# Second filter half transposed by the DMA engines instead of TensorE, and the first half's first inverse step cut into 64-row matmuls

## The chip, the cores and the metric

One core of one Trainium2 chip runs the whole program in one launch. The metric is the device time of one execution in microseconds (us), the median of several runs. The core has five instruction queues that run beside one another and meet only through semaphores: TensorE (PE, matmuls; its weight loads are listed apart as PEld), VectorE (DVE), ScalarE (ACT), GpSimd (POOL) and SyncE (SP), which here only issues DMA transfers. Each queue runs strictly in the order in which the program wrote it.

## What is computed

Two blocks, A and B, are each applied twice to an array x of 2048 rows and 512 channels that starts as `A_q`.

```python
def _A_ref(q, k, v, shift_k, ssm_k, ssm_D):
    k_shift = sum over t of k_pad[:, t:t + S, :] * shift_k[:, ks - 1 - t]     # 4 taps along the rows
    kv = k_shift * v
    y = irfft(rfft(kv padded to 2 S) * rfft(ssm_k padded to 2 S))[:S]         # causal convolution, per channel
    y = y + kv * ssm_D
    return q * y
x = x + _A_ref(_layernorm(x), A_k, A_v, A_shift_k, A_ssm_k, A_ssm_D)
x = x + _B_ref(_layernorm(x), B_w1, B_b1, B_w2, B_b2)     # layernorm, 512 -> 1376, gelu, 1376 -> 512
... the same two lines once more
```

Only `q` depends on x. The convolution result y depends on k, v and the filter `ssm_k` alone, so the kernel computes it once and uses it in both layers.

## The kernel before

**Two halves.** The 2048 rows are two halves of 1024. The program names things with `_0` and `_1` for the halves. y of the first half needs the first half of kv and the first half of the filter. y of the second half needs both halves of both. So the first half's y is ready early, and its two layers (13 smaller blocks of rows in all are worked through, 9 of them for the first half) run while the second half's convolution is still being computed.

**The convolution** is a Fourier transform written as matmuls, in two factors. The tags in the code are:

- `ht0`, `ht1`: the filter half, loaded with channels on the partitions, is turned so that rows lie on the partitions. `turn` (lines 556 to 568) does this: for each of four blocks of 128 channels, 8 TensorE transposes (line 561) into PSUM and one eviction by ACT or DVE.
- `h1_0`, `h1_1`: first factor of the filter's transform (`stage1`, lines 570 to 581): 8 tiles of 16 matmuls, weights of 64 columns, one eviction each (ACT or DVE).
- `h2_0`: second factor (`stage2`, line 590), 8 tiles. Each is evicted into the region HH, and `swap` (lines 594 to 601) copies HH with even and odd partitions exchanged into HI, by 8 DMAs of 256 KB on SP.
- `fir0` to `fir3`: the 4-tap filter of the first half, matmuls on a turned copy of k in region `R_KT`, times v (DVE, line 641).
- `x1_0`, `x2_0`: the two factors for kv, and the products with HH and HI (DVE, line 475, 16 instructions of 128x1024).
- `i1_0`, `i2_0`: the two inverse factors (`inverse1`, line 695; `inverse2`, line 717). `inverse1(..., split)` has two forms. Unsplit: per tile 16 matmuls with 128 rows of weights and 128 columns out. Split: 32 matmuls with 64 rows and 64 columns, two of them on different row halves of the array. The first half used the unsplit form, the second half (`i1_1`) the split one.
- `h2_1`, `p2`, `kt`, `fir4` to `fir7`, `x1_1`, `x2_1`, `sum`, `i1_1`, `i2_1`: the second half. `kt` turns k by 8 DMA transposes straight from DRAM (line 800).

**The layers** per block of rows: `q*` (statistics on DVE line 831, a small chain on POOL lines 836 to 846, a normalization on ACT line 856 or DVE line 857), `y*` (two DVE products and sums), `z*` (the same for the second layernorm, then a transpose, on TensorE for the first two blocks, by DMA after that, line 900), `m1` (line 920, gelu on ACT line 925), `m2` (line 954, added to x on DVE line 958).

**The order** is not found at run time. `SEQ` is a list of all 1187 operations in the order in which they are dealt to the engines' queues; `ENGS` holds one letter for every operation that may run on more than one engine; `BANKS` holds the PSUM bank of every tile. `arrange` reads the three, and `sync` sets the semaphore waits that the data need. A transfer in the SP queue that waits for its data holds back every transfer behind it.

The region `R_HP1`, which receives the turned second filter half, is the same memory as `R_KT`, so it may be written only after the `fir` matmuls of the first half have read it. `R_Y0` is written by `inverse2` of the first half and is free before.

Of the kernel before, what the change touches and what calls it, by code (L numbers as in the profile page):

```python
# [12 lines left out]
PE, ACT, DVE, POOL, SP = "tensor", "scalar", "vector", "gpsimd", "sync"  # L13
# [23 lines left out]
class Prog:  # L37
# [361 lines left out]
def bass_interleave_layers__ssm_conv_h3__mixer_channel_mlp__prompt_kernel(  # L399
        nc, A_q, A_k, A_v, A_shift_k, A_ssm_k, A_ssm_D, B_x, B_w1, B_b1, B_w2, B_b2, out):  # L400
    P = Prog(nc)
# [593 lines left out]
```

## Time and profile before

| | |
|---|---|
| time, median of 3 runs | 236.08 us (235.6 to 236.17) |
| profiled execution, first to last instruction | 234.0 us |
| granted TensorE clock, mean | 1.000 |
| PE busy | 222.7 us, 95% |
| DVE busy | 178.7 us, 76% |
| ACT busy | 164.5 us, 70% |
| POOL busy | 55.5 us, 24% |
| DMA queue of SP | 24.36 MB, 39.7% of 16 engines' span |

The page gives no other time for the profiled execution than its span; the median of the runs shown is 2.08 us above that span. Busy shares are averages over stages that have different limits, so they are read here by stretches of time. A PE that counts as busy isn't necessarily at its peak rate.

### The profile page before, as it was taken

How to read it: one execution, taken by the hardware profiler on the slowest of the kernel's cores; microseconds unless marked ns; L12 is line 12 of the kernel's file. 1: busy time of each engine (PE TensorE's matmuls, PEld its weight loads, DVE VectorE, ACT ScalarE, POOL GpSimd, SP SyncE). 2: the span in 40 equal slices, each digit the busy share in tenths (PEclk: the TensorE clock that was granted, in tenths of full speed). 3: DMA queues.
4: the chain of work that ended last, by engine and by line, in shares of the span. 5: the costliest groups of instructions: out<-in, count | busy, mean ns of one | idle time of the engine just before them, and what ended most of it. 6: DMA issues, size and time to landing. Idle time of an engine off the chain costs nothing.

```text
span 234.0 us, 6498 instructions
## 1 busy us (share of the span) xinstructions
PE 222.7 (95%) x2743; PEld 147.1 (63%) x2765; DVE 178.7 (76%) x362; ACT 164.5 (70%) x262; POOL 55.5 (24%) x113
## 2 busy tenths in 40 slices
PE   7989887999999999999999999999999999999995
PEld 3878776967868596677966576644444444444454
DVE  0699998999999999999999988781777569410222
ACT  2789999989968688999879986488058216802710
POOL 2270132006403405639303331204011120200000
PEclk9999999999999999999999999999999999999999
DMA  6999489928994360033500313401300130170202
GB/s 185 381 386 305 147 229 274 324 65 150 144 211 126 70 158 3 1 48 72 155 4 3 90 24 68 134 3 22 69 0 3 28 62 0 23 115 0 90 0 92
DMA packets 40106, 24.93 MB, mean 107 GB/s; under 512 B 23591, under 2 KB 33677, under 8 KB 40077
## 3 DMA queue, kind: packets, MB, share of 16 engines
q1 hardware_dynamic: 39778, 24.36, 39.7%
q8 instruction: 22, 0.36, 0.7%
q10 hardware_dynamic: 298, 0.16, 0.4%
q14 instruction: 8, 0.06, 0.1%
HBM read 13.23 MB, written 2.10 MB: 66 GB/s over the span
## 4 chain that ended last, share of the span: by engine, by line
PE 58%; DVE 24%; ACT 10%; issue 2%; POOL 2%; DMA 2%; SPq 0%; DVEq 0%
PE ps L920 23%; PE ps L954 23%; DVE ar L475 13%; ACT ar L480 9%; PE ps L695 4%; DVE sm L831 3%; PE ps L590 2%; DMA ar<-in_A_ssm_k_dram 2%; DVE ar L672 2%; DVE ar L958 2%; DVE ar L641 2%; PE ps L717 1%; POOL sm L836 1%; PE ps L578 1%; PE ps L635 1%
## 5 line engine op out<-in xcount | busy, mean ns | idle before, releaser
L925 ACT ACTIVATE ar<-ps,sm 128x256 bf16<-128x256 f32 (+5 forms) x143 | 65.7, 523 | 33.2 <-PE ps L920 32.9
L920 PE MATMUL ps<-ar 128*128 128x256 bf16 (+5 forms) x569 | 81.9, 297 | 0.4 <-ACT ar L480 0.2
L480 ACT ACTIVATE ar<-ps 128x1024 bf16<-128x1024 f32 (+3 forms) x77 | 71.1, 998 | 11.0 <-PE ps L578 3.4
L954 PE MATMUL ps<-ar 128*128 128x512 bf16 (+1 forms) x323 | 75.9, 379 | 1.5 <-issue 0.6
L920 PEld LDWEIGHTS ps<-ar 128*128 128x128 bf16 (+1 forms) x572 | 52.9, 100 | 27.5 <-ACT ar L480 1.1
L475 DVE TENSOR_TENSOR ar<-ar 128x512 bf16<-128x512 bf16 (+2 forms) x104 | 62.7, 646 | 1.5 <-ACT ar L480 0.8
L954 PEld LDWEIGHTS ps<-ar 128*128 128x128 bf16 (+1 forms) x341 | 32.4, 98 | 35.3 <-ACT ar L925 0.4
L958 DVE TENSOR_TENSOR ar<-ar,ps 128x512 bf16<-128x512 bf16 x31 | 20.8, 680 | 32.9 <-PE ps L954 32.9
L831 DVE BATCH_NORM_STATS2 sm<-ar 128x6 f32<-128x512 bf16 x64 | 42.5, 685 | 0.5
L856 ACT ACTIVATE ar<-ar,sm 128x512 bf16<-128x512 bf16 x39 | 30.6, 813 | 12.9 <-DVE sm L843 8.8
L836 POOL TENSOR_SCALAR sm<-sm 128x2 f32<-128x2 f32 (+2 forms) x22 | 9.9, 449 | 89.0 <-DVE sm L832 88.8
L838 POOL TENSOR_TENSOR sm<-sm 128x2 f32<-128x2 f32 (+2 forms) x26 | 21.7, 834 | 25.1 <-DVE sm L836 23.1
L590 PE MATMUL ps<-ar 128*128 128x64 bf16 x512 | 18.4, 193 | 1.5 <-DVE ar L481 0.7
L578 PE MATMUL ps<-ar 128*64 128x128 bf16 x512 | 17.9, 221 | 1.8 <-ACT ar L480 1.2
L590 PEld LDWEIGHTS ps<-ar 128*128 128x128 bf16 x512 | 16.8, 98 | 3.6 <-DVE ar L481 1.3
L578 PEld LDWEIGHTS ps<-ar 128*64 128x64 bf16 x512 | 14.9, 110 | 4.8 <-ACT ar L480 1.9
L481 DVE CAST ar<-ps 128x1024 bf16<-128x1024 f32 x12 | 14.6, 1218 | 1.2 <-PE ps L578 0.9
L846 POOL TENSOR_SCALAR sm<-sm 128x1 f32<-128x1 f32 x34 | 15.1, 460 | 1.6
L695 PE MATMUL ps<-ar 64*128 64x64 bf16 (+1 forms) x384 | 12.4, 203 | 1.0 <-DVE ar L475 0.9
L695 PEld LDWEIGHTS ps<-ar 64*128 64x128 bf16 (+1 forms) x384 | 11.8, 113 | 2.2 <-DVE ar L475 1.0
L857 DVE TENSOR_SCALAR ar<-ar,sm 128x512 bf16<-128x512 bf16 x25 | 10.3, 415 | 2.7 <-POOL sm L846 2.5
L788 DVE SCALAR_TENSOR_TENSOR ar<-ar,sm,ps 128x512 bf16<-128x512 bf16 x16 | 11.1, 740 | 0.3 <-PE ps L590 0.3
(45 smaller groups left out, 93.5 us busy)
## 6 DMA issues: line engine op xcount, KB each, us to landing
ar<-ar SPq DMA_DIRECT2D x16, 256.0 KB, 4.0
ar<-tab_s SPq DMA_DIRECT2D x9, 256.0 KB, 6.3
ar<-in_A_ssm_k_dram SPq DMA_DIRECT2D x8, 256.0 KB, 5.9
ar<-in_A_q_dram SPq DMA_DIRECT2D x8, 256.0 KB, 4.4
ar<-in_A_v_dram SPq DMA_DIRECT2D x8, 256.0 KB, 5.0
out_dram<-ar SPq DMA_DIRECT2D x7, 256.0 KB, 2.5
ar<-in_B_w_dram SPq DMA_DIRECT2D x4, 344.0 KB, 5.2
ar<-in_B_w_dram SPq DMA_DIRECT2D x5, 256.0 KB, 5.2
```

What stands on the lines that cost most here:

```text
L475: return P.op(eng, lambda e: e.tensor_tensor(o, a, b, op), dur, reads=[a, b] + list(more), writes=[o])
L480: return e.activation(dst, src(), AF.Copy)
L578: r = e.matmul(Q(tl, 64 * ri, 64, i * 128, [1, 128]), w, m, start=True, stop=True)
L590: r = e.matmul(Q(tl, 0, 128, i // 8 * 512 + i % 8 * 4, [32, 16], [1, 4]), w, m, start=True, stop=True)
L695: r = e.matmul(Q(tl, 0, 128, i, *([32, 16], [1, 4]) if split else ([1, 128],)), w, m, start=n == 0, stop=n == 1)
L831: P.op(DVE, lambda e, sj=sj, x=x: e.bn_stats(sj, x), 600.0, reads=[x], writes=[sj])
L838: P.op(POOL, lambda e: e.tensor_tensor(r, v, hf, ALU.pow), 420.0 + 149.0 * n, reads=[v, hf], writes=[r])
L856: return e.activation(o, x, AF.Identity, bias=u, scale=r)
L920: r = e.matmul(Q(tl, 0, rows, 0, [1, w]), a, m, start=dk == 0, stop=dk == 3)
L925: P.op(ACT, lambda e, dst=dst, tl=tl, rows=rows, bias=bias, w=w: e.activation(dst, Q(tl, 0, rows, 0, [1, w]), AF.Gelu_apprx_tanh, bias=bia ...
L954: r = e.matmul(Q(tl, 0, 128, 0, [1, 512]), ins[fc][0], ins[fc][1], start=fc == 0, stop=fc == 10)
L958: P.op(DVE, lambda e, x=x, tl=tl: e.tensor_tensor(x, x, Q(tl, 0, 128, 0, [1, 512]), ALU.add), 604.0, reads=[x], writes=[x], tile=tl)
```

## The change

Three things are changed.

1. **The second filter half is turned by DMA.** `load_h(1)` becomes 8 loads of 64 channels (128 KB each) instead of 4 of 128 channels, with the channels of a block dealt to the partitions in another order. The 32 TensorE transposes and four evictions of `ht1` go. In their place, POOL copies each block of 128 channels (128x1024) so that rows with the same remainder modulo 8 lie together, and 8 DMA transposes on SP (64x1024 each) turn the copies from `R_Y0` into `R_HP1`. The weights of `h1_1` are then read with a step of 8 elements between columns instead of 1.
2. **`i1_0` uses the split form.**
3. **One of the eight `spread` operations may run on POOL too, and `SEQ`, `ENGS` and `BANKS` are new.** There are now 1195 operations.

```diff
     def load_h(half, o):
         for b in range(4):
-            dma(A(0, 128, o + b * 1024, [1, 1024]), dr(A_ssm_k, b * 128 * 2048 + 1024 * half, [2048, 128], [1, 1024]), 1 << 18, paced=True)
+            if 1 and half:
+                for i in range(2):
+                    dma(A(64 * i, 64, o + b * 1024, [1, 1024]), dr(A_ssm_k, (b * 128 + 64 * i) * 2048 + 1024, [2048, 8], [8 * 2048, 8], [1, 1024]), 1 << 17, paced=True)
+            else:
+                dma(A(0, 128, o + b * 1024, [1, 1024]), dr(A_ssm_k, b * 128 * 2048 + 1024 * half, [2048, 128], [1, 1024]), 1 << 18, paced=True)
...
-            P.op(BOTH, f, {ACT: 912.0, DVE: 395.0}, reads=[c, m], writes=[o])
+            P.op((ACT, DVE, POOL), f, {ACT: 1040.0, DVE: 395.0, POOL: 2850.0}, reads=[c, m], writes=[o])
...
     load_h(1, R_HRAW1)
     P.tag = "ht1"
-    turn(1, R_HRAW1, R_HP1)
+    P.tag = "hcopy"
+    for b in range(4):
+        o, x = A(0, 128, R_Y0 + 1024 * b, [128, 8], [1, 128]), A(0, 128, R_HRAW1 + 1024 * b, [1, 8], [8, 128])
+        P.op(POOL, lambda e, o=o, x=x: e.tensor_copy(o, x), 2080.0, reads=[x], writes=[o])
+    P.tag = "ht1"
+    for b in range(4):
+        for i in range(2):
+            x, o = A(64 * i, 64, R_Y0 + 1024 * b, [1, 1024]), A(0, 128, R_HP1 + 1024 * b + 512 * i, [64, 8], [1, 64])
+            P.op(SP, lambda e, x=x, o=o: e.dma_start_transpose(o, x), 1300.0, reads=[x], writes=[o], dma=True, nbytes=1 << 17)
+    lhs = lambda g: A(0, 128, R_HP1 + 512 * (g // 8) + g % 8, [8, 64])
     P.tag = "h1_1"
-    stage1(lambda g: A(0, 128, R_HP1 + 64 * g, [1, 64]), R_G1)
+    stage1(lhs, R_G1)
...
     P.tag = "i1_0"
-    inverse1(R_1, R_2, R_3, False)
+    inverse1(R_1, R_2, R_3, 1)
```

The loads of the stage-two table and the `kt` transposes are rewritten (a variable `wide`, a function `turn_k`), with the same transfers as before.

**What the new lists say**, read off `SEQ` and `ENGS` (copies are numbered by block of 128 channels 0 to 3, transposes T0 to T7, two for each block):

- TensorE has 347 operations in its queue instead of 351 (an operation is a group of matmuls), SP 129 transfers instead of 117, POOL 103 instead of 91.
- SP: T7, one load of q, T6, T1, one small load; then seven of the eight `h2_0` swaps; T0, T4, T5; the eighth swap; then five loads, T2, T3, and the rest of the loads. Ahead of T7 stand 33 loads, as many as stood ahead of the first swap before; loads of block 0's two parts are the 25th and the 27th of them.
- POOL: ahead of the copies, the `taps` operations, one copy for `fir2`, one `spread`; then copy 3, copy 2, two small operations, copy 0; two operations of `q0`, two halo copies and two operations of `q1`; copy 1.
- TensorE: `h1_1` tile j needs T j. Tiles 6, 7, 1, 5, 4 stand ahead of `i1_0`, the same five as before; tiles 2, 3 and 0 behind it.
- DVE: 187 instructions up to the last `sum`, instead of 190. ACT: 54 up to and with the first gelu, instead of 57.

More of the change, by code (lines that the diff above doesn't have):

```diff
@@ L44 @@
     SEQ = (
[55 rows of a table removed]
[56 rows of a table added]
     ENGS = (
-            "pvavvvvvavpvpapapaaavaaaaavaavaavavvvppvvvaavvaaavaavvaaaaaaaaavaaaaavaaaavaaaaaaapppvaaaaaaaaaaaaaaaaaa"
-            "avaaaaaaaaapvapvvavpvppaappvvpvaavpaappaappaappaappaappavppvappaappaappvappaapvaapvavvavvvvvapvvvvvppvaa"
-            "avvvvaappavvapvavavpvvava")
+            "vvvvvapavvpavvpvvavaaaaaaavaaavaaavvvvvppvvavaaavaaaaaaaaavaaaaaaaavaavaaaaaaapvppaaaaaaaaaaaaaaaaaaaaaa"
+            "aaaaaaappvppavppvppaappvvppaappaappaavvaappaappaappaappaappaappaappvappvvppaappaavvpvavvapvvvvvppaaavppv"
+            "vvappaaavppvavappvvav")
     BANKS = (
-            "26624320240260660466027405640260464422140204626240406006442460424046462022442640460444626002206020640220"
-            "04023022660051677767117660640311026376367637332542537030213654742352762454741476061377362300423726574027"
-            "07315704314621527766215047034261015330227471565340011503350731745320154030276054756")
+            "20352024464606266226200312200640020644222406444026622002640642174064220004442424024406200442420200422443"
+            "34406617526445236756257634774021735435067763711652576007464673012336773166241304674325051735712336460047"
+            "5467457347732302713624571010542645124201731516341703502607235454057266742356401")
     def __init__(self, nc):
@@ L502, in load_t, with turn_k @@
             dma(A(0, 128, o + 512 * a, [1, 512 * w]), dr(x, 512 * (1024 * half + a), [8 * 512, 128], [1, 512 * w]), w << 17, paced=True)
-    tload(t_s2, 18432, 0, R_C, 1024)
+    wide = 18432
+    for h in range(1):
+        tload(t_s2, wide, 1024 * h, R_C + 1024 * h, 1024)
     load_h(0, R_1)
+    def turn_k(half):
+        for a in range(8):
+            src, dst = dr(A_k, 512 * (1024 * half + a), [8 * 512, 128], [1, 512]), A(0, 128, R_KT + 144 * a + 16, [1152, 4], [1, 128])
+            P.op(SP, lambda e, src=src, dst=dst: e.dma_start_transpose(dst, src), 1300.0, writes=[dst], dma=True, nbytes=1 << 17)
     load_t(A_k, 0, R_8, 2)
@@ L508, in bass_interleave_layers__ssm_conv_h3__mixer_channel_mlp__prompt_kernel @@
     for i in range(8, 16):
-        tload(t_s2, 18432, 2048 + i * 1024, R_S2 + i * 1024, 1024)
+        tload(t_s2, wide, 2048 + i * 1024, R_S2 + i * 1024, 1024)
     P.tag = "spread"
@@ L797, in bass_interleave_layers__ssm_conv_h3__mixer_channel_mlp__prompt_kernel @@
     P.tag = "kt"
-    for a in range(8):
-        src, dst = dr(A_k, 512 * (1024 + a), [8 * 512, 128], [1, 512]), A(0, 128, R_KT + 144 * a + 16, [1152, 4], [1, 128])
-        P.op(SP, lambda e, src=src, dst=dst: e.dma_start_transpose(dst, src), 1300.0, writes=[dst], dma=True, nbytes=1 << 17)
+    turn_k(1)
     for c in (0, 2):
```

111 rows, old and new, of the table SEQ are left out of this document.

## The prediction

> **What bounds the kernel now.** I read the busy times by stretch first, then the chain of work that ended last, then the groups by shape, last the SP queue. The stretches are cut where the chain changes its engine. Columns: stretch, its length, busy time and instructions of PE, PEld, DVE, ACT, POOL, granted clock, DMA share, GB/s.
>
> ```profile
> 12.00:28.00 16.00, 14.25 (x349) 12.35 (x349) 15.22 (x28) 14.68 (x16) 4.81 (x10) 1.00 0.91 298
> 28.00:42.00 14.00, 11.36 (x307) 10.20 (x306) 13.18 (x21) 13.83 (x16) 3.40 (x9) 1.00 0.82 233
> 42.00:56.00 14.00, 13.40 (x233) 11.07 (x232) 13.61 (x31) 12.79 (x16) 1.91 (x5) 1.00 0.66 167
> 56.00:124.00 68.00, 66.86 (x1054) 50.65 (x1061) 67.11 (x115) 59.20 (x116) 26.09 (x42) 1.00 0.43 93
> 124.00:234.00 110.00, 106.82 (x670) 55.49 (x679) 65.57 (x166) 57.83 (x96) 16.43 (x33) 1.00 0.19 44
> ```
>
> The page's 95% for PE hides two regimes. From 124 us on only PE is full (106.82 of 110), with DVE at 65.57. Before, PE, DVE and ACT are all nearly full: in 12 to 28 DVE has 15.22 of 16, in 28 to 42 ACT 13.83 of 14 while PE has 11.36, in 56 to 124 DVE 67.11 of 68. The chain (start, length, what) agrees:
>
> ```profile
> 41.32 7.39 PE ps L695 x128
> 48.73 6.59 ACT ar L480 x8
> ...
> 108.48 12.51 DVE ar L475 x11
> ...
> 124.17 1.67 PE ps L954 x7
> ```
>
> `i1_0` on PE follows DVE's products of `x2_0` (their row stands below), its evictions are ACT's, then the chain is mostly DVE up to 124, and PE's from there. So PE work taken out ahead of 124 pays only as far as DVE and ACT get there earlier; after 124 every PE microsecond pays, but the change touches no PE work there. Counted in the two orders, PE's queue holds 147 groups of matmuls from the first of `i1_1` on before and 148 after, all of `i1_1`, `i2_1`, `m1` and `m2`.
>
> **What each part takes away or adds.** The rows (count, busy us, mean ns of one):
>
> ```profile
> L695 PE MATMUL ps<-ar 128*128 128x128 bf16 x128 | 7.4, 219 | 0.9 <-DVE ar L475 0.9
> L695 PE MATMUL ps<-ar 64*128 64x64 bf16 x256 | 5.0, 194 | 0.1
> L561 PE MATMUL ps<-ar 128*128 128x128 bf16 x64 | 6.2, 252 | 0.6 <-DMA ar<-in_A_ssm_k_dram 0.3 <-ACT ar L480 0.3
> L610 PE MATMUL ps<-ar 128*128 128x128 bf16 x32 | 2.1, 219 | 0.0
> L561 PEld LDWEIGHTS ps<-ar 128*128 128x128 bf16 x64 | 5.3, 154 | 1.7 <-DMA ar<-in_A_ssm_k_dram 0.8 <-ACT ar L480 0.4 <-issue 0.3
> L610 PEld LDWEIGHTS ps<-ar 128*128 128x128 bf16 x32 | 1.8, 98 | 0.1
> 20.15 0.71 PE L561 MATMUL ps<-ar 128*128 128x128 bf16 x8
> 39.71 0.71 PE L561 MATMUL ps<-ar 128*128 128x128 bf16 x8 [0.28 <-ACT ar L480]
> L481 DVE COPY ar<-ps 128x1024 bf16<-128x1024 bf16 x7 | 4.8, 683 | 7.6 <-PE ps L561 6.9 <-PE ps L610 0.7
> L481 DVE CAST ar<-ps 128x1024 bf16<-128x1024 f32 x12 | 14.6, 1218 | 1.2 <-PE ps L578 0.9 <-PE ps L590 0.3
> L520 DVE TENSOR_SCALAR ar<-ar,sm 128x1024 bf16<-128x1024 bf16 x6 | 3.0, 512 | 0.0
> L857 DVE TENSOR_SCALAR ar<-ar,sm 128x512 bf16<-128x512 bf16 x25 | 10.3, 415 | 2.7 <-POOL sm L846 2.5
> L958 DVE TENSOR_TENSOR ar<-ar,ps 128x512 bf16<-128x512 bf16 x31 | 20.8, 680 | 32.9 <-PE ps L954 32.9
> L836 DVE TENSOR_SCALAR sm<-sm 128x4 f32<-128x4 f32 x2 | 0.3, 170 | 0.1
> L480 ACT ACTIVATE ar<-ps 128x1024 bf16<-128x1024 bf16 x5 | 5.2, 1037 | 2.6 <-PE ps L561 2.6
> L480 ACT ACTIVATE ar<-ps 128x1024 bf16<-128x1024 f32 x66 | 63.6, 1031 | 7.9 <-PE ps L578 3.4 <-PE ps L695 2.1 <-PE ps L717 1.7
> ```
>
> *PE.* The four `ht1` groups of 8 transposes (first and last shown) cost 4 x 0.71 = 2.8 us. `i1_0` falls from 7.4 us to what the split form takes in `i1_1`, 5.0: 2.4 us. Against that, `h1_1` now loads weights with a step of 8. Its nearest pair is `turn` (step 8) against `shift_turn` (step 1), both 128 columns: 6.2/64 = 97 ns against 2.1/32 = 66 per transpose, 31 ns more; half of it for 64 columns, 128 loads: 2.0 us. The ends are 0 (hidden behind the matmul) and half of 154 - 98 ns fully exposed, 3.6 us. I take 2.0, from the pace. Net -2.8 - 2.4 + 2.0 = -3.2 us.
>
> The Trainium skill, page "TensorE: Matmul & The Clock Gate", section "LDWEIGHTS (loading the stationary operand)", has the load's time follow the number of columns alone. By it the step costs nothing and PE's net would be -5.2 us; the 154 against 98 ns above, equal columns, speak against it.
>
> *DVE, to its last `sum`*, by the difference of the two queues (187 against 190 instructions): two `ht1` evictions -2 x 0.68; `h1_1` and `h2_0` one each fewer and `x1_0` one more, net -1.22; two second-norms -2 x 0.41; one `spread` -0.51; one `ht0` eviction +0.68; one addition to x +0.68; one `z` eviction of 512 columns, half of 0.68, +0.34; two single-row additions, bounded by the smallest row (0.17) and the 0.68 of a full eviction, nearest to the former but with more elements, 0.3 each, +0.6; net two tiny ones fewer, -0.3. Sum -1.9 us.
>
> *ACT, to its first gelu*: -2 x 1.04 (`ht1`), -1.04 (`ht0`), +1.03 (net one f32 eviction more), one z eviction fewer, about -0.6: -2.7 us.
>
> The three alternate on the chain, so the least counts: **-1.9 us**, as long as nothing new comes last. The candidates are POOL and SP.
>
> **What is late next.** Columns of the DMA rows: size, us to landing.
>
> ```profile
> 16.01 0.19 POOL L624 COPY ar<-ar 128x3 bf16<-128x3 bf16 x1
> L526 POOL MEMSET ar<- 128x512 bf16 x1 | 0.5, 524 | 0.1
> L548 POOL TENSOR_TENSOR ar<-ar 128x256 bf16<-128x256 bf16 x4 | 2.4, 612 | 3.3 <-DVE ar L481 3.1
> 27.22 1.23 DVE L481 CAST ar<-ps 128x1024 bf16<-128x1024 f32 x1 [0.33 <-PE ps L590]
> 16.96 3.36 SPq L470 DMA_DIRECT2D ar<-tab_s  x3
> 28.48 3.28 SPq L460 DMA_DIRECT2D ar<-ar  x4
> 33.25 3.21 SPq L460 DMA_DIRECT2D ar<-ar  x4
> 58.70 4.88 SPq L800 DMA_TRANSPOSE ar<-in_A_k_dram  x3
> 64.25 2.50 SPq L900 DMA_TRANSPOSE ar<-ar  x2
> ar<-ar SPq DMA_DIRECT2D x16, 256.0 KB, 4.0
> ar<-in_A_ssm_k_dram SPq DMA_DIRECT2D x8, 256.0 KB, 5.9
> 36.35 8.52 DVE L475 TENSOR_TENSOR ar<-ar 128x1024 bf16<-128x1024 bf16 x14 [0.82 <-ACT ar L480]
> ```
>
> POOL has no row for a 128x1024 copy. The ends are a memset's rate, 2 x 0.52 = 1.05 us, and a two-input product's, 4 x 0.61 = 2.45; I take 2.45, the nearer in that it reads the array, for the `spread` too. POOL is free of its early work at 16.2 (end of the halo copy at 16.01), so spread to 18.7, copies 3 and 2 to 23.6, two small operations, copy 0 to 26.4. A load of 256 KB lands 5.9 us after issue; block 0's last part is the 27th transfer, in the stretch that begins at 16.96, so issued at about 18.1 and landed by 24.0, just as copy 0 begins.
>
> An SBUF-to-SBUF transpose of as many bytes holds SP for 2.50/2 = 1.25 us; those from DRAM up to 4.88/3 = 1.63. A 64-row block has eight groups of 128 columns where the 128-row one has four, so the other end is 2.5; I take 1.25, the same bytes. T1 goes at 26.4 and ends at 27.7. The first swaps, which today wait for the eviction that ends at 28.45, have four instructions fewer ahead of them on DVE, but now start at 28.1. Seven swaps of 3.28/4 = 0.82 (5.7), T0, T4, T5 (3.75): the eighth swap is issued at 37.5 and lands 4.0 later, at 41.5. Four of the 16 products need it, and they are the last in DVE's order. Those products end today at 44.87; the DVE work ahead of them falls by 0.5 (of the terms above -1.36, -0.51, +0.68 and +0.6, a first norm moved ahead +0.41, tiny ones -0.3), so they would end at 44.4, and the last four begin at 44.4 - 4 x 0.61 = 41.9. So the swap lands 0.4 us in time. Behind it on SP wait T2, T3, half of the second inverse's table and most of B_w1; they are pushed from about 37 to 43 us to about 39 to 47, and with some 5 us to landing they are there by 52, ahead of the first `m1` at about 54. Behind T4 and T5 wait `h1_1` tiles 4 and 5, and behind those, in PE's order, `i1_0`: T5 ends on SP at 37.5 and must land by 41, which a landing as slow as the swaps' allows.
>
> The added DMA traffic (1 MB of transposes) falls into 22 to 43 us, where the DMA share is 0.82; it delays B's weights, which have the slack above.
>
> **The rivals.**
>
> *A. PE's saving counts in full.* If the searched order lets PE's 3.2 us through, 236.08 - 3.2 = 232.9; with free strided loads 230.9. Against it: DVE has 67.11 of 68 us in 56 to 124. Chance 0.12.
>
> *B. Nothing.* DVE's 1.9 us come out as waits, because `i1_0` still starts when the last products end, and the shortened queues are not the ones waited for: 236.1, within 0.3% (about what a measurement of this kernel can tell from no change). Chance 0.15.
>
> *C. The copies hold DVE.* Products and copies read SBUF at the same time, and one waits for the other. POOL does wait long here:
>
> ```profile
> 90.35 3.35 POOL sm L836
> ```
>
> One statistics operation on two to four columns took 3.35 us beside a full DVE. If it is DVE that waits, only copy 1, which follows at about 27.5 to 30, comes near the products (32.5 on): at most one copy, 2.45 us, minus 1.9: 236.6. Chance 0.05. The Trainium skill, page "SBUF — State Buffer", section "Who interferes with whom", has a two-input DVE instruction and a reading GpSimd instruction exclude each other for a whole instruction, whichever came first.
>
> *D. Slower: the eighth swap comes late.* It stands on SP behind six transposes, each of which waits for a copy on POOL. Each us beyond 0.4 goes through DVE into everything up to 124. It decides beyond 0.4 + 1.9 = 2.3 us of delay, that is transposes of 1.25 + 2.3/6 = 1.63 us, just what those from DRAM take at most. At 1.9, halfway between 1.25 and 2.5 us, the delay is 3.9, less 0.4 and 1.9: +1.6; if block 0's load also takes half as long again to land (2.9 us, for it runs when the DMA share is 0.91), +4.5. I price it between, 236.08 + 3.0 = 239.1. Chance 0.23. For it: the thin slack. Against it: equal bytes took 1.25 us twice. The Trainium skill, page "DMA: Bandwidth & Descriptors", section "Why a DMA increments its semaphore by 16 and not by 1", lets a DMA run on as many engines as divide its slowest dimension; the new loads' source has 8 there, so 8 engines of 16, and by an estimate twice the time to landing. No row of this case shows such a load.
>
> **The numbers.** Profiled span 234.0 - 1.9 = 232.1; with the 2.08 us by which the median exceeds the span, carried over, 234.2. Chances: forecast 0.45 (its own range 233.1 to 235.3), A 0.12, B 0.15, C 0.05, D 0.23. Faster by over 0.3% (below 235.37): forecast and A, 0.57. Within: B and most of C, 0.19. Slower: D and the rest, 0.24. The range takes A's nearer half and D up to a little above its price: 231.8 to 239.4.
>
> **What would show it.** No L561 in the second half's place and L695 at 256 more instructions and about 5.0 us less 7.4 each: right for PE. DVE's run of products ending near 44.4, `i1_0` near 47 instead of 48.7, the chain turning from DVE to PE near 122: the forecast. DVE idle ahead of the last four products, SP's transposes above 1.6 us, or POOL copies above 2.5: D. `h1_1`'s weight loads longer than 110 ns would settle the step of 8. The forecast is wrong if POOL or SP ends up on the chain before 45 us.

## The result, and the profile after

| | before | after |
|---|---|---|
| time, median | 235.98 us (235.6 to 236.17, 4 runs) | 244.5 us (243.19 to 248.22, 4 runs) |
| ratio to before, 95% interval | | 1.0332 (1.0305 to 1.0359) |
| span of the profiled execution | 234.0 us | 246.4 us |
| granted TensorE clock, mean | 1.000 | 0.972 |
| PE, DVE, ACT busy | 222.7, 178.7, 164.5 us | 225.2, 177.4, 165.6 us |
| start of the first `m1` | 56.46 us | 69.29 us |
| from there to the end of the span | 177.5 us | 177.1 us |

The change made the kernel slower, by 8.5 us between the medians and 7.8 by the ratio; the prediction was 234.2 us and its range ended at 239.4. The profiled execution of the changed kernel (248.22 us) is the longest of its four and was disturbed, like one of 327.23 us (granted clock 0.657) in the run with plain loads and weights, so the ratios leave both out and the trace below shows more loss than is usual. Its three other executions spanned 241.4 to 243.3 us; with the same 177.1 us behind the first `m1`, that would start at 64.3 to 66.2 there, by this estimate.

The last two rows of the table are the first thing to read. What comes after the first `m1` (the start of block B's first matmul) takes as long as before, to 0.4 us. The whole loss lies ahead of it. The stretches of the changed kernel, with the columns of the prediction's table (PE, PEld, DVE, ACT, POOL busy, granted clock, DMA share, GB/s):

```profile
12.00:28.00 16.00, 13.73 (x351) 12.07 (x350) 14.19 (x19) 12.01 (x14) 9.34 (x7) 1.00 1.19 260
28.00:42.00 14.00, 8.98 (x217) 8.46 (x217) 8.09 (x12) 8.37 (x10) 4.66 (x9) 0.88 0.81 160
42.00:56.00 14.00, 9.12 (x297) 8.59 (x293) 10.86 (x18) 10.52 (x12) 2.49 (x7) 0.76 1.03 206
```

From 28 to 42 DVE has 8.09 of 14 us where it had 13.18, ACT 8.37 where it had 13.83. No engine is full there any more. What they wait for, the chain of work that ended last tells (start, length, what; L589 is `stage1`, L706 `inverse1`, L763 the new transposes; "issue" is time in which the engine waits for nothing that the profile shows):

```profile
27.63 4.48 issue
...
41.22 1.69 SPq L763
...
42.95 1.27 SPq L763
...
44.26 4.36 DMA ar<-ar
...
48.66 2.18 PE ps L589 x32
50.84 4.48 PE ps L706 x199
55.32 2.68 issue
```

SP's queue is on the chain, with transposes T0, T4, T5 between 41.2 and 44.2; T5 lands at 48.6, and only then does TensorE get its last two early `h1_1` tiles and, behind them, `i1_0`, which starts at 50.84 instead of 41.32. Twice TensorE pauses for something that the profile doesn't name ("issue", 4.48 and 2.68 us). SP's own queue (start, length, line, transfer, count):

```profile
21.07 2.73 SPq L763 DMA_TRANSPOSE ar<-ar  x1
...
24.46 8.71 SPq L763 DMA_TRANSPOSE ar<-ar  x2
...
33.90 7.28 SPq L461 DMA_DIRECT2D ar<-ar  x7
41.22 4.31 SPq L763 DMA_TRANSPOSE ar<-ar  x3
45.57 1.11 SPq L461 DMA_DIRECT2D ar<-ar  x1
```

T6 and T1 hold SP from 24.46 to 33.17. Part of that is T1's wait for POOL's copy 0, which itself waited for its load (in brackets: idle time just before, and what ended it):

```profile
18.85 4.19 POOL L758 COPY ar<-ar 128x1024 bf16<-128x1024 bf16 x2 [2.20 <-DMA ar<-in_A_ssm_k_dram]
26.40 2.02 POOL L758 COPY ar<-ar 128x1024 bf16<-128x1024 bf16 x1 [2.83 <-DMA ar<-in_A_ssm_k_dram]
```

Copy 0 ends at 28.42; T1 then holds SP for up to 4.75 us more. The first swap starts at 33.90 instead of 28.48, the eighth at 45.57 instead of about 36. The share of the DMA engines between 24 and 34 us, in 40 slices, tenths:

```profile
DMA  9999979595555555559440099000109799921898
```

Until 26 us it is nearly full, and what is issued there lands late: the load of q issued at 23.84 takes 9.0 us, where 4.4 is the median of such loads before. From 26.2 to 28.5 it stands at one half, and from 28.75 to 31.5 the engines are mostly idle. So it is not full DMA engines that hold T1 for 4.75 us. That long hold belongs to this execution: the run with plain `h1_1` weights below has the same order on SP, and there T1 leaves SP at 28.36, 1.2 us after copy 0.

### The profile page after: what moved, and what is told of

Read it like the earlier page. It is cut to its first block, busy times and chain, and to the rows that moved or that the text cites. A ratio compares the mean times of both kernels' runs of the same rounds, so it can differ in the third digit from the quotient of the medians.

```text
span 246.4 us, 6745 instructions
## 1 busy us (share of the span) xinstructions
PE 225.2 (91%) x2861; PEld 147.9 (60%) x2861; DVE 177.4 (72%) x352; ACT 165.6 (67%) x260; POOL 66.5 (27%) x138
## 4 chain that ended last, share of the span: by engine, by line
PE 82%; DMA 6%; SPq 5%; issue 3%; DVE 2%; ACT 2%; DVEq 0%
PE ps L938 31%; PE ps L972 30%; PE ps L589 6%; PE ps L601 5%; DMA ar<-in_A_v_dram 4%; PE ps L706 4%; SPq L461 3%; PE ps L728 3%; DMA ar<-ar 2%; ACT ar L481 2%; SPq L763 1%; PE ps L961 1%; PE ps L674 1%; PE ps L646 1%; DVE ar L482 1%
## 5 line engine op out<-in xcount | busy, mean ns | idle before, releaser
L481 ACT ACTIVATE ar<-ps 128x1024 bf16<-128x1024 f32 (+2 forms) x75 | 70.8, 998 | 23.7 <-PE ps L601 8.6
L943 ACT ACTIVATE ar<-ps,sm 128x256 bf16<-128x256 f32 (+4 forms) x143 | 66.3, 524 | 29.8 <-PE ps L938 29.5
L938 PE MATMUL ps<-ar 128*128 128x256 bf16 (+4 forms) x572 | 81.6, 297 | 0.6 <-DVE ar L482 0.6
L972 PE MATMUL ps<-ar 128*128 128x512 bf16 (+1 forms) x341 | 79.0, 379 | 0.0
L476 DVE TENSOR_TENSOR ar<-ar 128x512 bf16<-128x512 bf16 (+3 forms) x106 | 63.7, 631 | 6.8 <-ACT ar L481 4.3
L849 DVE BATCH_NORM_STATS2 sm<-ar 128x6 f32<-128x512 bf16 x64 | 42.7, 682 | 0.6
L589 PE MATMUL ps<-ar 128*64 128x128 bf16 x512 | 22.8, 244 | 8.8 <-issue 4.5
L589 PEld LDWEIGHTS ps<-ar 128*64 128x64 bf16 x512 | 19.5, 137 | 11.6 <-issue 5.3
L864 POOL TENSOR_SCALAR sm<-sm 128x1 f32<-128x1 f32 x54 | 18.2, 356 | 2.3
L706 PE MATMUL ps<-ar 64*128 64x64 bf16 x512 | 10.2, 200 | 2.7 <-issue 2.7
L706 PEld LDWEIGHTS ps<-ar 64*128 64x128 bf16 x512 | 9.6, 115 | 4.2 <-issue 3.2
```

What stands on the lines that cost most here:

```text
L476: return P.op(eng, lambda e: e.tensor_tensor(o, a, b, op), dur, reads=[a, b] + list(more), writes=[o])
L481: return e.activation(dst, src(), AF.Copy)
L589: r = e.matmul(Q(tl, 64 * ri, 64, i * 128, [1, 128]), w, m, start=True, stop=True)
L706: r = e.matmul(Q(tl, 0, 128, i, *([32, 16], [1, 4]) if split else ([1, 128],)), w, m, start=n == 0, stop=n == 1)
L849: P.op(DVE, lambda e, sj=sj, x=x: e.bn_stats(sj, x), 600.0, reads=[x], writes=[sj])
L938: r = e.matmul(Q(tl, 0, rows, 0, [1, w]), a, m, start=dk == 0, stop=dk == 3)
```

## The experiments

All ratios are to the kernel before, run beside them on the same chip (medians 235.98 to 236.44 us). "First swap" is its issue time on SP, "rest" is the span less the start of the first `m1`; all times in us. The last three columns are of the one execution that was profiled, which need not be a typical one: it took 248.22 us for the changed kernel, 237.38 with the loads of 8 and 235.95 with the 6 behind swaps and tables. The run with plain loads and weights has no trace that compares.

| kernel | time | ratio, 95% interval | first swap | first `m1` | rest |
|---|---|---|---|---|---|
| before | 235.98 | 1 | 28.48 | 56.46 | 177.5 |
| changed | 244.5 | 1.0332 (1.0305 to 1.0359) | 33.90 | 69.29 | 177.1 |
| before, 6 idle transposes among the swaps | 240.66 | 1.0187 (1.0160 to 1.0214) | 29.00 | 61.22 | 177.4 |
| before, the 6 behind the swaps | 239.3 | 1.0117 (1.0071 to 1.0162) | 29.16 | 60.41 | 177.5 |
| before, the 6 behind swaps and tables | 236.88 | 1.0030 (1.0008 to 1.0053) | 28.87 | 56.67 | 177.5 |
| before, loads of 8 (outermost dimension 8) | 238.86 | 1.0107 (1.0060 to 1.0153) | 29.78 | 57.98 | 177.6 |
| changed, plain loads | 242.37 | 1.0276 (1.0229 to 1.0323) | 30.42 | 65.17 | 177.1 |
| changed, loads over 128 partitions | 244.23 | 1.0335 (1.0275 to 1.0395) | 30.99 | 62.58 | 180.0 |
| changed, plain `h1_1` weights | 242.32 | 1.0254 (1.0213 to 1.0296) | 29.08 | 63.53 | 177.4 |
| changed, plain loads and weights | 242.75 | 1.0254 (1.0208 to 1.0301) | | | |
| before, `i1_0` split | 237.95 | 1.0028 (0.9990 to 1.0065) | 28.30 | 58.67 | 177.4 |
| changed, TensorE's transposes back | 239.18 | 1.0128 (1.0104 to 1.0153) | 26.10 | 60.15 | 177.4 |
| the same, `i1_0` unsplit: new order alone | 240.08 | 1.0153 (1.0123 to 1.0183) | 27.27 | 61.33 | 177.5 |
| changed, in the order of before | 243.36 | 1.0296 (1.0264 to 1.0327) | 33.66 | 64.52 | 177.5 |
| changed, swaps first | 249.87 | 1.0600 (1.0559 to 1.0641) | 26.63 | 70.02 | 177.2 |
| changed, swaps and tables first | 250.86 | 1.0597 (1.0558 to 1.0636) | 26.32 | 71.47 | 177.1 |
| changed, swaps, tables and q first | 244.7 | 1.0363 (1.0327 to 1.0399) | 26.09 | 66.11 | 177.1 |
| changed, early transposes later | 245.0 | 1.0394 (1.0343 to 1.0445) | 26.21 | 65.83 | 177.2 |
| before, one block by DMA | 236.81 | 1.0034 (1.0016 to 1.0052) | 28.99 | 57.55 | 177.6 |
| the same, tables first | 237.13 | 1.0051 (1.0026 to 1.0076) | 28.90 | 57.46 | 177.4 |

With one exception the rest is 177.1 to 177.6 us, whatever was done: the start of the first `m1` decides the time.

### What a transpose costs by where it stands on SP

Three kernels put six transposes that nobody reads into the kernel before, each of the shape of the change, and differ only in their place. The order on SP (S is a swap, T a transpose; other loads are left out):

```diff
-S S S S   S S S   S   table  table
+T  T T  S S S S   S S S  T T T  S   table  table     (among the swaps)
+S S S S   S S S S   T T T T T T   table  table       (behind the swaps)
+S S S S   S S S S   table table   T T T T T T        (behind the tables too)
```

> The kernel before, whole, with six DMA transposes added that nobody reads: 64 partitions by 1024 of the raw second half into free room, of the shape of the change, three on SP ahead of the first swap and three ahead of the eighth; no POOL copy, no 8-engine load. Theory S: the first swaps wait behind 3 transposes (1.3 to 2.5 us each) and the eighth behind 6, so the last swap lands 6 to 10 us later, TensorE runs dry ahead of i1_0, and the time is 239 to 243 us. If transposes cost little where the rings are not backed up by half-width loads: 236 to 238 us, and the cost needs both.

It took 240.66 us. SP's queue:

```profile
24.75 2.92 SPq L743 DMA_TRANSPOSE ar<-ar  x2
29.00 3.35 SPq L455 DMA_DIRECT2D ar<-ar  x4
34.10 2.32 SPq L455 DMA_DIRECT2D ar<-ar  x3
36.47 4.86 SPq L743 DMA_TRANSPOSE ar<-ar  x3
41.38 0.61 SPq L455 DMA_DIRECT2D ar<-ar  x1
```

The three early ones delay the first swap by only 0.5 us; the three ahead of the eighth swap put its issue at 41.38, and the first `m1` comes 4.76 us later. So theory S, that the place on SP costs, holds in size. Whether the traffic would cost the same elsewhere was the next question.

> The kernel before with the same six idle DMA transposes as in the run that put three ahead of the first swap and three ahead of the eighth (that one took 240.66 us, first m1 at 61.22 instead of 56.46), but with all six behind the eighth swap on SP. Theory S (the cost is that the transposes hold SP's queue ahead of the swaps): swaps and i1_0 as in the kernel before, first m1 near 56.5 to 57.5, 236 to 237.5 us; what stands behind the six, weights and the remaining q, comes 8 us later and is not needed at once. Rival L (transposes slow the rest of the DMA traffic wherever they stand): 239 to 241 us again.

239.3 us, which is what the rival expected. But the chain of its profiled execution says why (L743 transposes, L465 the table loads, L712 `i2_0`):

```profile
37.13 1.65 SPq L743
...
45.92 0.58 SPq L465
...
49.38 5.55 DMA ar<-tab_small
...
55.06 2.59 PE ps L712 x8
```

The second table of `i2_0` stood behind the six. It was issued at 49.38 us instead of 40.75, landed at 54.9, and `i2_0` waited for it. The next thing in the queue had become the victim.

> As the run with six idle DMA transposes behind the eighth swap (239.3 us; there the second table for i2_0 was issued at 49.38 instead of 40.75 and TensorE waited for it), but with the two table loads moved ahead of the six, so that what stands behind them is weights alone. Theory S (a transpose costs what its 1.3 us on SP delay in the next thing that is needed): i2_0 no longer waits, first m1 near 56.5 to 57.5, 236 to 237.5 us. Rival L (it costs by its traffic): 239 us again.

236.88 us, ratio 1.0030. The same six transposes, the same traffic:

```profile
33.65 3.19 SPq L455 DMA_DIRECT2D ar<-ar  x4
36.88 1.22 SPq L465 DMA_DIRECT2D ar<-tab_small  x2
38.15 8.42 SPq L743 DMA_TRANSPOSE ar<-ar  x6
46.62 3.02 SPq L455 DMA_DIRECT2D ar<-in_B_w_dram  x5
```

They still hold SP for 8.42 us, but only weights wait behind them, and those have time. So in the kernel before, what six transposes cost goes by their place on SP: 4.4, 2.8 or 0.7 us by the ratios. The place also moves the hour of their traffic; that it is the delay on SP rests on the two chains as well, which run through SP's transposes to the eighth swap in the first run and to the table in the second. The earlier tables are no hidden gain: in the kernel before, nothing on TensorE waits for them.

### The loads

```diff
-dr(A_ssm_k, (b * 128 + 64 * i) * 2048 + 1024, [2048, 8], [8 * 2048, 8], [1, 1024])
+dr(A_ssm_k, (b * 128 + 64 * i) * 2048 + 1024, [2048, 64], [1, 1024])
```

> The changed kernel with one edit: the eight loads of the second filter half read 64 consecutive channels each, so that the source's outermost dimension counts 64 and not 8; bytes, order and everything behind are the same, the channels of a group land on other partitions (that part of the output differs). Theory K (a load whose outermost dimension counts 8 runs on 8 of the 16 DMA engines; their backlog holds the copies, SP and a fetch of TensorE's instructions): the time falls from about 244 to 233-236.5 us, the wait of copy 0 for its load (2.8 us) and TensorE's pauses without a releaser (4.5 and 2.7 us) go, the DMA share in 24 to 30 us isn't stuck near a half. Rival R (the 64-row transposes and the copies themselves hold SP): the time stays at 242 us or more.

242.37 us: 2.1 us less than the changed kernel by the medians, 1.3 by the ratios, whose intervals overlap, so the gain is not clear of noise; and far from 236.5. Copy 0 waited 1.44 us for its load instead of 2.83, but TensorE's pauses did not go (3.48, 1.55 and 2.11 us). These loads still cover 64 partitions each. The other way round, the kernel before with its four loads dealt as the change deals them (`[2048, 8], [8 * 2048, 16], [1, 1024]`):

> The kernel before with one edit: its four loads of the second filter half read the channels in an order whose outermost dimension counts 8 (that part of the output differs). No copy and no DMA transpose waits for them. Theory K: 3 to 8 us slower than before (239-244), with a stretch in which half of the DMA engines are busy and a TensorE pause without a releaser. Rival R: within 0.7 us of before (235.3-236.7).

238.86 us, +2.5 by the ratio. So the loads cost 2.5 us in the kernel before; in the changed kernel their price is not shown. A third form covers all 128 partitions with 16 rows of the outermost dimension and half the columns:

> The changed kernel, computing the reference: each block's channels are dealt in an order whose outermost dimension counts 16, by two loads of all 128 partitions and 512 rows each, and the weights of h1_1 are read from the places that follow. A tile of h1_1 now needs both transposes of its block; one kt transpose stands a few places later. Theory K: 233-236.5 us. Rival R: 242 or more.

244.23 us. POOL's copies barely waited and the first `m1` came at 62.58, but this form needs both transposes of a block for each tile and moved one `kt` transpose back, and the second half's swaps came onto its chain: the rest grew to 180.0 us. It says nothing on the loads alone.

### The step in the weights

```diff
-lhs = lambda g: A(0, 128, R_HP1 + 512 * (g // 8) + g % 8, [8, 64])
+lhs = lambda g: A(0, 128, R_HP1 + 64 * g, [1, 64])
```

> The changed kernel with the h1_1 weights read without a step (the same 512 columns for every tile, 64 neighbours at a time), nothing else; the second half's part of the output is altered by it. In the traces a stepped h1_1 tile takes 1.17 us at the full clock, one of the kernel before 0.64, and four of the eight stand on the chain of the changed kernel (two before i1_0 and two or three behind it). Theory W (the step of 8 costs 0.53 us a tile and is paid where the chain runs through TensorE): 241.5 to 243 us. If the chain's waits absorb it: 243.5 to 244.5 us.

242.32 us, 1.8 us less by the ratios: theory W. The size is read at a granted clock of 1.00. First the groups by shape of the kernel before, from 36 to 62 us (weight loads of `h1_1`: count, busy us, mean ns), then one tile in its timeline:

```profile
L578 PEld LDWEIGHTS ps<-ar 128*64 128x64 bf16 x112 | 3.3, 110 | 1.3 <-ACT ar L480 0.8 <-issue 0.4
```

```profile
36.63 0.64 PE L578 MATMUL ps<-ar 128*64 128x128 bf16 x16
```

The same two views of the changed kernel with swaps, tables and q first:

```profile
L583 PEld LDWEIGHTS ps<-ar 128*64 128x64 bf16 x126 | 7.9, 215 | 4.2 <-ACT ar L475 3.7 <-issue 0.4
```

```profile
58.26 1.17 PE L583 MATMUL ps<-ar 128*64 128x128 bf16 x16 [0.69 <-ACT ar L475]
```

A stepped load takes 215 ns instead of 110, a tile 1.17 us instead of 0.64: 0.53 x 8 = 4.2 us of TensorE.

> As the run with plain loads over 16 engines (242.37 us), with the h1_1 weights read without a step as well; the second half's part of the output is altered by both. If loads and step are separate prices that add: 239.5 to 241 us, which leaves 3.5 to 5 us for the transposes' place on SP, the copies and the new order. If one hides the other: 241.5 us or more.

242.75 us, by the interval no better than either alone: one price hides the other, or the sum is too small to be told.

### The order, and the split `i1_0`

```diff
-inverse1(R_1, R_2, R_3, False)
+inverse1(R_1, R_2, R_3, True)
```

> The kernel before with i1_0 in the split form alone. If time ahead of 124 us is set by DVE and ACT as the prediction has it, TensorE's 2.4 us are mostly hidden: 235 us (234.5-236.2). If they count in full: 233.6.

237.95 us, interval 0.999 to 1.0065, with executions from 234.67 to 239.29: no gain shown. Next, the changed kernel with its four TensorE groups and evictions back and no copies, DMA transposes or step:

> The changed kernel's new order with the old way of turning: the second filter half is loaded by four 128-partition DMAs and turned by TensorE (four groups of eight transposes and four evictions, put back ahead of the h1_1 tiles that need them), the POOL copies and DMA transposes are gone, the h1_1 weights are contiguous; i1_0 stays in 64-row tiles. Theory S and rival L both put the loss on the new way of turning: 235 to 238 us. Theory O (the newly searched order itself, say later first loads or a worse order of the early stages, is what costs): 241 us or more.

239.18 us. So by the ratios 4.8 of the 7.8 us go with the new way of turning, and 3.0 remain in an order that was made without these evictions. With `i1_0` unsplit as well:

> The new order alone: as the run that put TensorE's transposes back into the changed kernel (239.18 us), with i1_0 in full tiles as in the kernel before. If the new order itself costs 2 to 3 us: 238 to 239.5 us. If the split i1_0 cost it there: 236 to 237 us, as in the kernel before.

240.08 us, in line with the new order costing by itself. (The two differ by 0.9 us in favour of the split form, and their intervals overlap.) And the change without its order:

> The whole change without its new order: eight half-block loads over 8 engines, POOL copies, DMA transposes, stepped h1_1 weights and the split i1_0, put into the order of the kernel before; on SP one transpose stands ahead of the last load before the swaps, two ahead of the first swap, two ahead of the eighth, three behind it, and the load that fills part of the copies' room follows these. Theory S plus 8-engine loads (2.5 us by the run on those, 4.2 us by the one on idle transposes, less what TensorE, VectorE and ScalarE get back from the transposes and evictions that are gone, 1 to 3 us): 239 to 243 us, TensorE idle ahead of i1_0. If the newly searched order is what costs most: 237 us or less. If the order had saved time: 245 us or more.

243.36 us, TensorE idle ahead of `i1_0`. The new order is neither the cause nor the cure: by the ratios the change costs 7.0 us without it and 7.8 with it, and the intervals overlap. The order alone cost 3.0 to 3.6, so the parts do not add. In this run TensorE has no unexplained pause above 0.4 us between 10 us and the first `m1`.

### The same in the changed kernel

Each of the next four changes the order on SP alone, save for the `h1_1` tiles that have to follow their transposes (5 of them behind `i1_0` in the first three) and for POOL's fourth copy, which the second and third move ahead of its other work:

```diff
-T7 T6 T1  S x7  T0 T4 T5  S  ... table ... T2 T3 ... table     (changed)
+S x8  T x6  ...                                               (swaps first)
+S x8  table table  small load  T x8  q ...                    (swaps and tables first)
+S x8  table table  small load  q  T x8 ...                    (swaps, tables and q first)
+S x7  T x6  S  ...                                            (early transposes later)
```

> The changed kernel with its order altered in one point: the six DMA transposes that stood ahead of the eighth swap of the spectrum on SP (T7, T6, T1, T0, T4, T5) stand behind all eight swaps, and the five h1_1 tiles that TensorE worked on before i1_0 stand behind i1_0; all that is computed stays. Theory S (what costs time is that transposes hold SP's queue while the swaps, the products and i1_0 wait): the swaps start near 28.5 to 30.5 us and the last one lands near 41 instead of 49.9, i1_0 starts near 42, and what is left is the price of the 8-engine loads (2 to 2.5 us by the two runs on those): 237 to 240 us. Rival L (the transposes and half-partition loads slow everything that the DMA engines carry wherever they stand, and TensorE's pauses come with that): 242 to 245 us, with pauses of TensorE without a releaser of 3 us and more still there.

249.87 us, a miss, by its own order: T2 and T3 had stayed behind five loads on SP, at 46.35, and landed at 53, and the second `h1_1` tile behind `i1_0` needed T3. (The copies that the next text names had ended at 32.1; they were not what it waited for.) Mended:

> The changed kernel in whole, its order altered: behind the eight swaps stand the two table loads and the small load that POOL waits for, then all eight DMA transposes, with the five early h1_1 tiles behind i1_0 as in the run that put the swaps first (249.87 us, where copies on POOL stood behind that small load) and the fourth POOL copy ahead of POOL's other work. Theory S: the last transpose lands near 50 instead of 53.15, no pause of 2 us on TensorE before i1_0, first m1 between 60 and 64 instead of 69.3, 239 to 242 us; what stays is the 8-engine loads and five h1_1 tiles and their evictions that now stand behind i1_0. Rival L: 244 us or more.

250.86 us, a miss again, and again the chain names the load that had moved behind the eight:

```profile
47.30 1.98 SPq L757
49.32 4.04 DMA ar<-in_A_q_dram
...
53.99 0.40 DVE ar L869
54.39 1.14 DVE ar L476
55.58 3.14 PE ps L583 x48
```

A normalization on DVE waits for the last q load, an eviction stands behind it on DVE, and TensorE's `h1_1` waits for that: DVE is busy 0.62 us between 48 and 54.

> The run with swaps and tables first (250.86 us; there TensorE, out of work from 49 to 55, waited for the last q load, which stood behind the eight DMA transposes and was issued at 49.32), with that one load moved ahead of the eight transposes. If a transpose costs what it delays in the next needed thing: that wait ends, the h1_1 tiles start near 50 instead of 55.58, and first m1 comes 4 to 6 us before 71.5: 245 to 247 us. If the time follows the DMA traffic: 250 us or more again.

244.7 us: one 256 KB load moved ahead of eight transposes is worth 6.2 us by the medians, 5.5 by the ratios. This is the mechanism at its plainest. But it is no better than the changed kernel, and its chain shows what the early transposes had bought:

```profile
42.15 3.62 PE ps L700 x116
...
49.62 5.01 PE ps L583 x80
```

`i1_0` starts at 42, nearly as in the kernel before, but five `h1_1` tiles of 1 us that used to fill TensorE while the swaps ran now follow it.

> The changed kernel with one alteration: T7, T6 and T1, which stood ahead of the first swap, stand behind the seventh, in front of T0, T4 and T5; the h1_1 tile of T6 moves three groups back on TensorE, to the other early h1_1 tiles. The six are still ahead of the eighth swap. If early transposes cost, by holding SP ahead of the first swap and by TensorE's pause of 4.5 us that begins as they are issued: the first swap near 27 instead of 33.9, no pause there, the eighth swap near 41 instead of 45.57, 240 to 242.5 us. If the early transposes only move the wait to the eighth swap: 243.5 to 245.5 us.

245.0 us: the wait moved to the eighth swap and to T's landing, as the second case said. The first pause of TensorE shrank from 4.5 us to 1.2; the second stayed (2.58):

```profile
40.83 1.27 SPq L757
42.14 3.44 DMA ar<-ar
...
45.63 2.18 PE ps L583 x25
47.81 4.33 PE ps L700 x219
52.13 2.58 issue
```

### A version to beat both

> A version that may beat both: the kernel before with one block of the four turned by DMA, the one whose two h1_1 tiles stand behind i1_0. Its load keeps 128 partitions, one POOL copy follows it, its two DMA transposes stand on SP behind the eighth swap, its group of eight TensorE transposes and its eviction (on ScalarE) go; the two h1_1 tiles take stepped weights. By theory S nothing is held: TensorE loses 0.71 us and pays 0.25 us for each stepped tile, ScalarE loses one eviction of 0.93 us in a stretch in which it is nearly full: 235.2 to 236.2 us. By rival L two more transposes cost 1 to 1.5 us: 236.5 to 238 us.

236.81 us, ratio 1.0034 (1.0016 to 1.0052): slower by a little. Its tables stood behind two transposes, so:

> As the run with one block of four turned by DMA (236.81 us against 236.07), but with the two table loads ahead of its two transposes on SP. Theory S: the two transposes then delay only weights, i2_0 starts as in the kernel before, and the eviction and the 0.71 us of TensorE that are gone show: 235.3 to 236.2 us. If the two stepped h1_1 tiles and the copy cost what is gained: 236.5 to 237 us again.

237.13 us, no better. In the first of the two `i1_0` starts at 41.54, 0.2 us late, and the first `m1` at 57.55, 1.1 us late; between them stand its two stepped tiles, 0.53 us longer each, which is about the difference (by the timeline; no run took the step away here). None of these versions beats the kernel before.

## Why the prediction was wrong

**What bounds the kernel.** Right: PE, DVE and ACT full in turn until 124 us, PE after that. But the cut that matters is the first `m1` at 56: what lies behind it took 177.1 to 177.6 us in all kernels but one. Savings had to show as an earlier first `m1`, and there the chain goes swap, products, `i1_0`, which no term of the sum made earlier.

**PE's terms.** The transposes' 2.8 us are gone as said. The split `i1_0` keeps its predicted pace where nothing holds it (64 of its 256 matmuls in 1.25 us in the run with TensorE's transposes back), but in the kernel before it brought no time. The step of 8 was mis-sized: 2.0 us taken, 3.6 as the upper end, 4.2 measured. Half of 154 - 98 ns per load, 28 ns, was the end; the load took 105 ns more. The Trainium skill's page "TensorE: Matmul & The Clock Gate", section "LDWEIGHTS (loading the stationary operand)", by which the columns alone count, is contradicted here by 215 against 110 ns at 64 columns each. With 4.2 in place of 2.0 the saving on PE falls from 3.2 to 1.0 us.

**DVE and ACT.** The 1.9 us were given under the condition that nothing new comes last. Something did, so they appear as waits: DVE is busy 177.4 us instead of 178.7 and stands idle for 5.9 of the 14 us from 28 to 42.

**What is late next: the step that failed.** Single pieces of the walk along SP's list were right: POOL's copies took 2.02 us (2.45 taken), a transpose that waited for nothing 1.27 us (1.25 taken). Its sum was not: "the eighth swap is issued at 37.5 and lands 4.0 later, at 41.5", 0.4 us ahead of the products that need it. In the profiled execution it was issued at 45.57, partly because of T1's long hold. The run with plain `h1_1` weights shows the same order on SP without that hold (SP's queue, then pieces of the chain):

```profile
23.08 5.28 SPq L763 DMA_TRANSPOSE ar<-ar  x2
29.08 8.78 SPq L461 DMA_DIRECT2D ar<-ar  x7
37.91 4.77 SPq L763 DMA_TRANSPOSE ar<-ar  x3
...
26.55 4.60 issue
...
42.72 3.76 DMA ar<-ar
46.51 2.51 DVE ar L476 x4
```

The first swap comes at 29.08 instead of 28.1, the seven swaps hold SP for 8.78 us instead of 5.7, and T0, T4, T5 for 4.77 instead of 3.75. So the eighth is issued at 42.72 and lands at 46.5, and the last four products start at 46.51 instead of 41.9. The largest error is the seven swaps. They were counted at their bare duration, but a swap also waits for the eviction of its `h2_0` tile; on the chain of this run these evictions stand behind TensorE's pause of 4.60 us. The sentence "T5 ends on SP at 37.5 and must land by 41, which a landing as slow as the swaps' allows" failed with it: T5 ended at 42.7 and landed at 44.2 in this run, at 44.2 and 48.6 in the profiled execution of the changed kernel. The slack of 0.4 us was the difference of long sums of estimates, each taken at its undisturbed duration. The signs named for this came: SP stood on the chain before 45 us, and DVE idled ahead of the last four products (1.24 us, and 0.33 with plain weights).

**The rivals.** A and B did not happen. C was not put to the test: copy 1 ended at 32.9, before the products began, and the sixteen products take 682 ns each after and 688 before. D had the sign and the place, the eighth swap that comes late. Of its two terms the slow transposes were too large (1.9 us each taken; the three ahead of the eighth swap took 4.77 together), and the slow half-block load was smaller too: copy 0 began 1.1 us late with plain weights and 2.4 in the profiled execution, where 2.9 was taken. Its price of 3.0 us was still too small, for it lacked the swaps' wait, the step in the weights, paid where the chain runs through `h1_1` (1.8 us by its run), and TensorE's pauses and slow clock. The loads' 8 engines of 16, which the Trainium skill's page "DMA: Bandwidth & Descriptors" gave in the section "Why a DMA increments its semaphore by 16 and not by 1", agree with +2.5 us in the kernel before, and with the stretch at one half of the DMA engines from 26.2 to 28.5 us above; no row here shows the single engines. The runs give 2.5 us for the loads in the kernel before, 1.8 for the weights, 3 for the new order and up to 4.4 for the transposes' place; these overlap and are no sum of the 7.8.

**Open.** Why TensorE paused, and how much of the loss its two pauses are, was not settled. Pauses of 2 us and more came only in the changed order, the longest while T6 and T1 were being issued, and moving those shortened the first without making the kernel faster. The change in the order of before had none of them and lost 7.0 us all the same.

## What to carry to other kernels

Work moved from a busy engine to the DMA side is not free when one queue issues all transfers: a transpose that nobody reads cost 0.1 us or 0.7 us each, by what stood behind it. Before such a move, list what is next in the issuing queue for each new entry and when it is needed, and count each entry with the wait for its own data, not at its bare duration. And find first the point behind which everything keeps its length (here the first `m1`): only what makes that point earlier saves time.

## What was not expected of the hardware

- Weights read with a step of 8 elements load in 215 ns instead of 110 (64 columns), at the full clock.
- TensorE's granted clock is lower after an idle stretch: it stood from 44.9 to 48.7 us, then had 0.50 to 51 and 0.76 to 54 while it worked, and 1.00 after that, so an idle stretch is paid again. With plain weights it had 0.59 from 30 to 33, after the pause of 4.60. The prediction left this out, though the Trainium skill's page "TensorE: Matmul & The Clock Gate", section "Part 1: The HAM clock gate", has the clock halve after an idle window; the 0.50 below agrees. In the changed kernel (columns as above, the clock third from the end):

```profile
30.00:33.00 3.00, 0.89 (x14) 0.72 (x15) 0.12 (x1) 0.00 (x0) 2.73 (x3) 0.83 0.84 102
33.00:36.00 3.00, 3.00 (x71) 3.00 (x69) 1.56 (x2) 1.94 (x2) 0.27 (x1) 0.60 0.54 50
36.00:39.00 3.00, 2.09 (x67) 1.85 (x64) 3.00 (x6) 2.98 (x4) 0.00 (x0) 1.00 0.81 228
...
48.00:51.00 3.00, 2.34 (x42) 2.23 (x44) 1.76 (x4) 1.08 (x2) 0.12 (x1) 0.50 0.90 173
51.00:54.00 3.00, 3.00 (x158) 3.00 (x154) 1.61 (x3) 3.00 (x4) 0.69 (x2) 0.76 1.21 289
```

- TensorE can stand for 4.48 us in the middle of a tile with nothing to wait for that the profile shows. The DMA queues from 24 to 34 us show one packet of the instruction queue that took 3.9% of the 16 engines' time, some 6 us of one engine. A fetch of instructions that came late would explain the pause, but no run tested that:

```profile
q8 instruction: 1, 0.02, 3.9%
```
